# Moving the start of the projection phase two slots earlier in a fused threshold-attention and hard-swish kernel

## The chip, the cores and the metric

The kernel runs on one core of one Trainium2 chip. A core has five engines that run side by side and wait for one another through semaphores: TensorE (PE in the profile, its weight loads PEld), VectorE (DVE), ScalarE (ACT), GpSimd (POOL) and SyncE (SP, which here only issues transfers). The metric is the device time of one execution in microseconds (us). Less is better.

## What is computed

Threshold attention over 8 batches of 8 heads, 576 rows and 64 columns, and on its output, seen as 4608 tokens of 512 features, two projections with a hard-swish between them.

```python
scores = scale * np.matmul(q, k.transpose(0, 1, 3, 2))
thresh = np.max(scores, axis=-1, keepdims=True) - tau
scores = np.where(scores >= thresh, scores, -1000000000.0)
attn   = softmax(scores)                      # exp, divided by the sum of its row
x      = np.matmul(attn, v)                   # (8, 8, 576, 64) -> (4608, 512)
h      = x @ w_in                             # 512 -> 2048
g      = h * np.clip(h + 3.0, 0.0, 6.0) / 6.0
out    = g @ w_out                            # 2048 -> 512, float32
```

## The kernel before

The attention is cut into 16 groups of four heads ("quads", two pairs of heads each). A quad has nine slots. Slots 0 to 3 are 128 query rows of the first pair, 4 to 7 of the second pair, and slot 8 takes the last 64 rows of both. So there are 144 slots, n = 0 to 143, and one loop runs over them. In slot n each engine gets a share of a pipeline that is several slots deep:

- `scores(m)`: PE multiplies q and k in float32 into PSUM for a slot ahead.
- `sm_max(m)`: DVE copies the two score tiles out of PSUM and takes the row maxima; `sm_bias` on POOL makes the threshold.
- `sm_mask`, `sm_exp`: ACT masks and exponentiates, two instructions each for the two heads.
- `sm_recip` (DVE) and `sm_norm` (POOL): the quotient, in bfloat16, tile `pn`.
- the transposed `pn`: by `pe_transpose` where the slot is marked `on_chip` (nine PE instructions and a DVE copy), else by a DMA transpose that SP issues.
- `multiply(n)`: the products with v, on PE, and their copies `xT`, `xR` on DVE.
- `mm1(item)`: one piece of the first projection, eight PE instructions of 256 columns (or four of 512), and after it the rectifier `mm1_relu` (ACT in even slots, DVE in odd ones) and the gate `mm1_gate` (DVE).
- `second()`: pieces of the second projection. Four pieces of four PE instructions of 512 columns make one output tile of 128 tokens.

`N1` is the slot from which projections are done in the loop. There also the scores change from one slot at a time to bursts of two slots, in odd slots. Up to `N2` the exponentials of an even slot stand ahead of the rectifier on ACT.

```python
    N0 = 3
    N1 = 22
    N2 = 28
    HB, OB = 6, 7                 # PSUM banks of the two projections
    ...
    def bank():                   # two "small" banks, in turn: transposes and products with v
        nonlocal turn
        turn += 1
        return ps[:, (2, 5)[turn % 2], :]

    def copy_out(out, in_):
        if 0 <= now <= N1:
            nc.vector.tensor_copy(out=out, in_=in_)
        else:
            nc.scalar.copy(out=out, in_=in_)
    ...
    def first(n):                 # odd slots of the burst phase have score columns of their own
        return n > N1 + 2 and n % 2
    def score_col(n, a):
        return (704 if first(n) else 128) + (0 if a else 1536)
    ...
            sl.on_chip = len(queue) < N1 - 1 and (slot in (1, 3, 5, 7, 8) or slot == 0 and quad > 0)
    ...
    turns = {1: [("q", 1)], 2: [("k", 1)], 3: [("rest", 0)]}     # transposes of q and k by slot
    ...
        if quad < NB:             # NB = 2: when the products with v of the first two quads are done
            jobs = ((8, p0, 0, 512), (13 - 2 * quad, p1, 0, 512), (15 - 3 * quad, None, 0, 0))
        else:
            jobs = [(7 - quad % 2 + 2 * i, *of) for i, of in enumerate(
                ((p0, 0, 256), (p0, 256, 256), (p1, 0, 256), (p1, 256, 256), (None, 0, 0)))]
        for after, *of in jobs:
            products.setdefault(quad * NSLOT + after, []).append((quad, *of))

    def multiply(n):              # finished products bring pieces of the first projection into todo1
        copies = []
        for of, pair, *columns in products.get(n, ()):
            copies.append(av_rest(of) if pair is None else av_main(pair, *columns))
            if of % 2 and pair is None:
                todo1.extend(moe_of(of // 2)[1])
            elif pair == 2 * of + 1 and of % 2 and columns[0] == 0:
                todo1.extend(moe_of(of // 2)[0])
        return copies

    def second():
        nonlocal pieces, bb, mt, part
        pieces = 2 if now % 2 == 0 and todo2 else 0
        for _ in range(pieces):
            bb, mt, part = todo2.pop(0)
            mm2_part(bb, mt, part)
    ...
    for n, sl in enumerate(queue):
        ...
        if 0 < n <= N1: (exponentials of the slot before)
        if n <= N1 or n > N2 + 1 or n % 2 == 0: sm_max(queue[n + 1])
        even = n >= N1 and n % 2 == 0
        ...
        if N0 <= n <= N1: scores(n + 2)
        if even and n <= N2: sm_max(queue[n + 2])
        exp_first = even and n <= N2
        ...
        if todo1 and n >= N1:
            item, then = todo1.pop(0)
            ...
            h = mm1(item, 0 if n == len(queue) - 1 else OB if n > N1 and n % 2 and not pieces else HB)
            todo2.extend(then)
        ...
        elif n > N1 and n % 2:
            for m in (n + 3, n + 2): scores(m)
        ...
        if n < 4 or 15 < n < 20 or n > 33:
            start(vcasts, 1 if n < N1 or n % 2 else 0)
        else:                     # transfers of w_in and w_out, 32 pieces, issued by POOL
            start(casts, 2 if n in (5, 8, 11, 14) or 21 < n < 28 else 1)
    ...
    def last_out():               # the last output tile, one PSUM bank, two halves
        osb = o_pool.tile([P, d_model], F32, tag="osb", name="osb")
        r0, c = B * S - 64 - P, d_model // 2
        nc.scalar.activation(out=osb[:, 0:c], in_=o_ps[0][:, 0:c], func=Act.Copy, scale=1.0 / 6.0)
        nc.scalar.dma_start(out=out[r0:r0 + P, 0:c], in_=osb[:, 0:c])
        nc.vector.tensor_scalar_mul(out=osb[:, c:2 * c], in0=o_ps[0][:, c:2 * c], scalar1=1.0 / 6.0)
        nc.sync.dma_start(out=out[r0:r0 + P, c:2 * c], in_=osb[:, c:2 * c])
```

After the loop comes a tail: the pieces of both projections that are left over, most of them of the last batch, whose attention is only then complete.

Of the kernel before, what the change touches and what calls it, by code (L numbers as in the profile page):

```python
# [9 lines left out]
F32 = mybir.dt.float32  # L10
# [3 lines left out]
Act = mybir.ActivationFunctionType  # L14

P = 128
# [4 lines left out]
def kernel(  # L21
# [10 lines left out]
    nc = tc.nc  # L32
    B, H, S, D = q.shape
# [6 lines left out]
    NSLOT = 9  # L40
    NB = 2
    N0 = 3
    N1 = 22
    N2 = 28
    HB, OB = 6, 7
    scale = 1.0 / math.sqrt(D)
    tau = float(tau)
# [35 lines left out]
    def load_quad(quad):  # L83
        b, g = divmod(quad, 2)
        nat[quad] = (nat_pool.tile([P, 1152], F32, tag="nq", name="nq"),
                     nat_pool.tile([P, 4, 4, D], F32, tag="km", name="km"),
                     nat_pool.tile([P, 2 * D], F32, tag="kr", name="kr"))
        nq, km, kr = nat[quad]

        def main(dst, src, h, order, by=nc.sync):  # L90
            by.dma_start(out=dst[:, :, h, :], in_=src[b, 4 * g + h, 0:512, :].rearrange(order, t=4))

        def blocks_q(n, a, j):
            c = 32 * (2 * a + j)
            nc.sync.dma_start(out=nq[c:c + 32, n * S:(n + 1) * S].rearrange("p (k d) -> p k d", d=32),
                              in_=q[b, 4 * g + 2 * n + a, :, 32 * j:32 * j + 32].rearrange("(k r) d -> r k d", r=32))

        def blocks_k(n, a, j):
            c = 32 * (2 * a + j)
            nc.sync.dma_start(  # L100
                out=km[c:c + 32].rearrange("p t h d -> p (t h d)")[:, n * 512:(n + 1) * 512].rearrange(
                    "p (t m d) -> p t m d", t=4, d=32),
                in_=k[b, 4 * g + 2 * n + a, 0:512, 32 * j:32 * j + 32].rearrange("(m r t) d -> r t m d", r=32, t=4))

        def load_k(n):
            if b < NB:
                for a in range(2):
                    main(km, k, 2 * n + a, "(p t) d -> p t d")
            else:
                for a in range(2):  # L110
                    for j in range(2):
                        blocks_k(n, a, j)

        def load_q(n):
            if b < NB:
                for a in range(2):
                    main(nq[:, 0:1024].rearrange("p (t h d) -> p t h d", h=4, t=4), q, 2 * n + a, "(t p) d -> p t d",
                         by=nc.scalar if quad == n == 0 else nc.sync)
            else:
                for a in range(2):  # L120
                    for j in range(2):
                        blocks_q(n, a, j)

        def rest():
            for dst, src in ((kr[:], k), (nq[:, 1024:1152], q))[0:2 if b < NB else 1]:
                for n in range(2):
                    (nc.sync if b < NB else nc.gpsimd).dma_start(out=dst[64 * n:64 * n + 64, :].rearrange("p (h d) -> p h d", h=2),
                                      in_=src[b, 4 * g + 2 * n:4 * g + 2 * n + 2, 512:S, :].rearrange("h p d -> p h d"))

        def both():  # L130
            rest()
            load_k(1)

        if b < NB:
            loads.extend((lambda: load_k(0), lambda: load_q(0), rest, lambda: load_k(1), lambda: load_q(1)))
        else:
            loads.extend((lambda: load_q(0), lambda: load_k(0), lambda: load_q(1), both))
# [34 lines left out]
    def start(jobs, n):  # L172
        for _ in range(min(n, len(jobs))):
            jobs.pop(0)()
# [42 lines left out]


    def copy_out(out, in_):
        if 0 <= now <= N1:  # L220
            nc.vector.tensor_copy(out=out, in_=in_)
        else:
            nc.scalar.copy(out=out, in_=in_)  # L223
# [46 lines left out]
        return evict  # L270

    def first(n):
        return n > N1 + 2 and n % 2

    def score_col(n, a):
        return (704 if first(n) else 128) + (0 if a else 1536)
# [98 lines left out]
    def mm1(item, hb=HB):  # L375
        b, ni, c0 = item
        if c0 is None:
            for ki in range(KI):
                nc.tensor.matmul(ps[:, hb, :], xR[b // 2][:, ki, :], w_in_sb[:, ki, ni * P:ni * P + 512],  # L379
                                 start=(ki == 0), stop=(ki == KI - 1))  # L380
        else:
            for n in range(2):
                for ki in range(KI):
                    nc.tensor.matmul(ps[:, hb, n * 256:(n + 1) * 256], w_in_sb[:, ki, (ni + n) * P:(ni + n + 1) * P],  # L384
                                     xT[b][:, ki, c0:c0 + 256], start=(ki == 0), stop=(ki == KI - 1))
        return ps[:, hb, :]
# [27 lines left out]
    def mm2_part(bb, mt, part, ob=OB):  # L414
        if part == 0:
            o_ps[0] = ps[:, ob, :]
        for ni in range(part * 4, part * 4 + 4):
            nc.tensor.matmul(o_ps[0], gbuf[:, ni, mt * P:(mt + 1) * P], w_out_sb[:, ni, :],  # L418
                             start=(ni == 0), stop=(ni == NI - 1))
# [55 lines left out]
    for quad in range(NQUAD):  # L475
        for slot in range(NSLOT):
            sl = Slot()
            sl.quad, sl.slot, sl.n = quad, slot, len(queue)
            sl.on_chip = len(queue) < N1 - 1 and (slot in (1, 3, 5, 7, 8) or slot == 0 and quad > 0)
            queue.append(sl)  # L480
    scores(0)
    sm_max(queue[0])
    sm_bias(queue[0])
    scores(1)

    turns = {1: [("q", 1)], 2: [("k", 1)], 3: [("rest", 0)]}

    def turn_at(n, job, of):
        turns.setdefault(n, []).append((job, of))
# [10 lines left out]
    for quad in range(NQUAD):  # L500
        p0, p1 = 2 * quad, 2 * quad + 1
        if quad < NB:
            jobs = ((8, p0, 0, 512), (13 - 2 * quad, p1, 0, 512), (15 - 3 * quad, None, 0, 0))
        else:
            jobs = [(7 - quad % 2 + 2 * i, *of) for i, of in enumerate(
                ((p0, 0, 256), (p0, 256, 256), (p1, 0, 256), (p1, 256, 256), (None, 0, 0)))]
        for after, *of in jobs:
            products.setdefault(quad * NSLOT + after, []).append((quad, *of))
# [10 lines left out]

    def second():  # L520
        nonlocal pieces, bb, mt, part
        pieces = 2 if now % 2 == 0 and todo2 else 0
        for _ in range(pieces):
            bb, mt, part = todo2.pop(0)
            mm2_part(bb, mt, part)
# [5 lines left out]
    for n, sl in enumerate(queue):  # L531
# [45 lines left out]
        if todo1 and n >= N1:  # L577
            item, then = todo1.pop(0)
            if n == len(queue) - 2:
                second()  # L580
            h = mm1(item, 0 if n == len(queue) - 1 else OB if n > N1 and n % 2 and not pieces else HB)
            todo2.extend(then)
        else:
            item = None
# [61 lines left out]
        if n < 4 or 15 < n < 20 or n > 33:  # L646
            start(vcasts, 1 if n < N1 or n % 2 else 0)
        else:
            start(casts, 2 if n in (5, 8, 11, 14) or 21 < n < 28 else 1)
        prev = sl  # L650

    last = NQUAD - 1
    count = [1, 0 if todo2 and todo2[0][2] else 1]


    def last_out():
        osb = o_pool.tile([P, d_model], F32, tag="osb", name="osb")
        r0, c = B * S - 64 - P, d_model // 2
        nc.scalar.activation(out=osb[:, 0:c], in_=o_ps[0][:, 0:c], func=Act.Copy, scale=1.0 / 6.0)
        nc.scalar.dma_start(out=out[r0:r0 + P, 0:c], in_=osb[:, 0:c])  # L660
        nc.vector.tensor_scalar_mul(out=osb[:, c:2 * c], in0=o_ps[0][:, c:2 * c], scalar1=1.0 / 6.0)
        nc.sync.dma_start(out=out[r0:r0 + P, c:2 * c], in_=osb[:, c:2 * c])

    def rest1(item, then, on_act=True):
        h = mm1(item, hb=(0, 1, 3, 4)[count[0] % 4])
# [4 lines left out]
    def rest2():  # L670
        while todo2:
            bb, mt, part = todo2.pop(0)
            mm2_part(bb, mt, part, ob=OB - count[1] % 2)
            if part == 3:
                flush()
                if (bb, mt) == (B // 2 - 1, 8):
                    last_out()
                else:
                    late.extend(mm2_out(bb, mt, on_act=(count[1] % 2 == 0)))
                count[1] += 1  # L680

    av_main(2 * last + 1, 0, 256)()
# [50 lines left out]
```

## Time and profile before

| | |
|---|---|
| time, median of 3 runs | 516.75 us (516.36 to 516.82) |
| span of the profiled execution | 515.1 us |
| PE, PEld busy | 504.9, 318.6 us |
| DVE, ACT, POOL busy | 441.9, 451.8, 300.4 us |
| first and last reciprocal of the slot loop | 14.99 us, 469.15 us |

How to read it: each slot from 1 on does one reciprocal on DVE (`sm_recip` of the slot before), and one more follows the loop, so the starts of the 144 reciprocals cut the span into slots. The one done in slot n starts slot n in the tables of this document: slot 20 begins at 67.71 us, slot 22 at 73.53, slot 30 at 99.52, slot 36 at 119.69 and slot 46 at 151.66. The loop then ends near 469 us, and the rest is the tail. A busy share of the whole span mixes three stages (softmax alone, softmax with projections, projections alone), so the windows by slot say more than the totals. PE's busy time is modelled from the sizes of its instructions and counts overlapping ones once, so 100% does not mean that no more work would fit.

### The profile page before, as it was taken

What the parts mean: (1) busy time and instruction counts of PE and PEld (TensorE: products, weight loads), DVE (VectorE), ACT (ScalarE), POOL (GpSimd) and SP (SyncE); (2) the same over time, 40 slices, a digit from 0 to 9 for tenths busy, and PEclk for the clock granted to TensorE, in tenths of its full rate; (3) what the DMA queues carried; (4) which work ended last, traced back from release to release, by engine and by line L of the source; (5) the groups of instructions that cost most, each with busy time, mean ns of one, the idle gap of its engine ahead of it and who ended that gap; (6) DMA issues with size and microseconds to landing.
All of it is one profiled execution on the core that took longest, in us unless ns stands there. A gap on an engine that the chain in (4) does not pass through costs nothing.

```text
span 515.1 us, 12094 instructions
## 1 busy us (share of the span) xinstructions
PE 504.9 (98%) x4127; PEld 318.6 (62%) x4127; DVE 441.9 (86%) x1124; ACT 451.8 (88%) x980; POOL 300.4 (58%) x538
## 2 busy tenths in 40 slices
PE   8999999999999999999999999999999999999997
PEld 6655566566655666666655666666655666667563
DVE  3698898998999999999999999999999999887260
ACT  3999989999999999999999999999999999986060
POOL 0788888756666666666566756657566655552000
PEclk9999999999999999999999999999999999999999
DMA  6998999989999999999898999999999997655132
GB/s 140 163 175 140 157 148 178 160 141 176 164 195 157 173 164 170 179 176 174 164 178 143 183 169 160 159 170 168 164 173 176 183 181 114 115 111 81 74 63 61
DMA packets 314094, 78.77 MB, mean 153 GB/s; under 512 B 296624, under 2 KB 309168, under 8 KB 314032
## 3 DMA queue, kind: packets, MB, share of 16 engines
q1 hardware_dynamic: 294464, 67.90, 79.8%
q0 software_dynamic: 18368, 9.71, 15.6%
q8 instruction: 32, 0.52, 0.4%
q10 hardware_dynamic: 1200, 0.39, 0.3%
q14 instruction: 30, 0.25, 0.2%
HBM read 36.70 MB, written 9.44 MB: 90 GB/s over the span
## 4 chain that ended last, share of the span: by engine, by line
PE 79%; ACT 5%; DVE 2%; issue 0%
PE ps L288 24%; PE ps L418 24%; PE ps L384 20%; PE ps L349 7%; PE ps L379 3%; ACT s L317 2%; ACT s L312 2%; PE ps L352 1%; ACT r L392 1%; DVE g L407 1%; DVE r L394 0%; PE ps L340 0%; DVE s L303 0%; ACT kT L223 0%; PE ps L258 0%
## 5 line engine op out<-in xcount | busy, mean ns | idle before, releaser
L325 POOL TENSOR_SCALAR pn<-s,rinv 128x576 bf16<-128x576 f32 x288 | 211.4, 746 | 18.9 <-issue 4.8
L303 DVE TENSOR_SCALAR_CACHE_REDUCE s<-ps 128x576 f32<-128x576 f32 x288 | 205.0, 748 | 16.4 <-PE ps L288 8.3
L312 ACT ACTIVATE s<-s,bias 128x576 f32<-128x576 f32 x288 | 205.8, 762 | 5.1 <-POOL bias L308 4.7
L317 ACT ACTIVATE s<-s 128x576 f32<-128x576 f32 x288 | 192.4, 670 | 0.3
L288 PE MATMUL ps<-kT,qT 64*128 64x384 f32 (+7 forms) x1280 | 175.4, 419 | 3.9 <-DVE s L303 2.4
L288 PEld LDWEIGHTS ps<-kT,qT 64*128 64x128 f32 (+1 forms) x1280 | 102.9, 175 | 60.3 <-issue 15.8
L418 PE MATMUL ps<-w_out_sb,g 128*128 128x512 bf16 x576 | 134.1, 379 | 0.0
L384 PE MATMUL ps<-xT,w_in_sb 128*128 128x256 bf16 x1024 | 130.9, 273 | 0.8 <-DVE g L407 0.8
L384 PEld LDWEIGHTS <-w_in_sb 128*128 128x128 bf16 x1024 | 95.6, 98 | 40.7 <-issue 21.7
L308 POOL TENSOR_SCALAR bias<-m 128x2 f32<-128x2 f32 x144 | 27.1, 188 | 150.5 <-DVE rinv L320 135.6
L407 DVE SCALAR_TENSOR_TENSOR g<-r,ps 128x512 bf16<-128x512 f32 x128 | 87.8, 687 | 15.0 <-ACT r L392 10.8
L418 PEld LDWEIGHTS <-g 128*128 128x128 bf16 x576 | 56.2, 98 | 56.8 <-issue 0.4
L392 ACT ACTIVATE r<-ps,three 128x512 f32<-128x512 f32 x81 | 55.5, 686 | 24.7 <-PE ps L384 20.5
L317 ACT ACTIVATION_READ_ACCUMULATOR s<-s 128x1 f32 x288 | 54.4, 189 | 0.0
L394 DVE TENSOR_SCALAR r<-ps 128x512 f32<-128x512 f32 x63 | 42.9, 680 | 0.0
L349 PE MATMUL ps<-pT,vm 128*64 128x256 bf16 (+1 forms) x480 | 39.1, 285 | 0.0
L349 PEld LDWEIGHTS <-vm 128*64 128x64 bf16 x736 | 27.2, 110 | 16.1 <-issue 14.6
L360 DVE CAST xT<-ps 128x256 bf16<-128x256 f32 (+1 forms) x60 | 26.2, 436 | 10.2 <-PE ps L352 10.2
L426 DVE TENSOR_SCALAR osb<-ps 128x512 f32<-128x512 f32 x31 | 20.9, 673 | 8.4 <-PE ps L418 8.4
L303 DVE DVE_READ_ACCUMULATOR s<-ps 128x1 f32 x288 | 23.8, 83 | 0.0
L320 DVE RECIPROCAL rinv<-rsum 128x2 f32<-128x2 f32 x144 | 23.0, 159 | 0.6 <-ACT s L317 0.6
L144 POOL DMA_DIRECT2D vm<-in_v_dram x28 | 21.5, 768 | 0.7 <-issue 0.6
(57 smaller groups left out, 253.9 us busy)
## 6 DMA issues: line engine op xcount, KB each, us to landing
out_dram<-osb SPq DMA_DIRECT2D x31, 256.0 KB, 2.7
nq<-in_q_dram SPq DMA_DIRECT2D x96, 72.0 KB, 3.4
km<-in_k_dram SPq DMA_DIRECT2D x96, 64.0 KB, 3.4
vm<-in_v_dram POOLq DMA_DIRECT2D x24, 128.0 KB, 4.3
km<-in_k_dram SPq DMA_DIRECT2D x16, 128.0 KB, 4.1
w_in_sb<-in_moe_w_in_dram POOLq DMA_DIRECT2D x16, 128.0 KB, 3.6
w_out_sb<-in_moe_w_out_dram POOLq DMA_DIRECT2D x16, 128.0 KB, 4.2
pT<-pn SPq DMA_TRANSPOSE x117, 4.0
```

The lines of the kernel that those rows point to most:

```text
L288: nc.tensor.matmul(ps_flat[rows, c0:c0 + w], qT_of(pair)[a * 64:(a + 1) * 64, q0:q0 + rows.stop - rows.start], kT_of(pair)[a * 64:(a + 1) ...
L303: nc.vector.tensor_scalar(out=sl.s[:, i, :], in0=ps_flat[:, c0:c0 + S], scalar1=1.0, scalar2=None, op0=Alu.mult, op1=Alu.max, accum_out=sl ...
L308: nc.gpsimd.tensor_scalar(out=sl.bias[:], in0=sl.m[:], scalar1=-scale, scalar2=tau, op0=Alu.mult, op1=Alu.add)
L312: nc.scalar.activation(out=s, in_=s, func=Act.Prelu, bias=sl.bias[:, i:i + 1], scale=scale, alpha=REJECT)
L317: nc.scalar.activation(out=s, in_=s, func=Act.Exp, accum_out=sl.rsum[:, i:i + 1])
L325: nc.gpsimd.tensor_scalar(out=pn[:, i, :], in0=sl.s[:, i, :], scalar1=sl.rinv[:, i:i + 1], scalar2=1.0, op0=Alu.mult, op1=Alu.mult)
L349: nc.tensor.matmul(pb[a * 64:(a + 1) * 64, :], vm[:, 2 * hp + a, c * D:(c + 1) * D], pT[:, 5 * a + c, cols], start=(c == 0), stop=False)
L384: nc.tensor.matmul(ps[:, hb, n * 256:(n + 1) * 256], w_in_sb[:, ki, (ni + n) * P:(ni + n + 1) * P], xT[b][:, ki, c0:c0 + 256], start=(ki = ...
L392: nc.scalar.activation(out=r, in_=hps, func=Act.Relu, bias=three[:])
L394: nc.vector.tensor_scalar(out=r, in0=hps, scalar1=3.0, scalar2=0.0, op0=Alu.add, op1=Alu.max)
L407: nc.vector.scalar_tensor_tensor(out=out, in0=r, scalar=6.0, in1=hps, op0=Alu.min, op1=Alu.mult)
L418: nc.tensor.matmul(o_ps[0], gbuf[:, ni, mt * P:(mt + 1) * P], w_out_sb[:, ni, :], start=(ni == 0), stop=(ni == NI - 1))
```

## The change

It starts the burst scheme and the first projection in slot 20 in place of 22, and moves what hangs on it: the limit `N2`, the set of slots that are transposed on chip, the products of the second quad (one of them now in two halves), the rate at which the weights are fetched, and the number of pieces of the second projection in slots 36 to 44. Three further edits are independent of that: the k transpose of pair 1 moves from slot 2 to slot 1, the tail rows of k for quad 4 are fetched from SP's queue and not from POOL's, and the last output tile is computed as two halves of 256 columns in two PSUM banks. The purpose is to give PE projection work earlier, while the loop is still held up by the softmax.

```diff
-    N1 = 22
-    N2 = 28
+    N1 = 20
+    N2 = 26
...
-                    (nc.sync if b < NB else nc.gpsimd).dma_start(out=dst[64 * n:64 * n + 64, :] ...
+                    (nc.sync if quad < 5 else nc.gpsimd).dma_start(out=dst[64 * n:64 * n + 64, :] ...
...
     def copy_out(out, in_):
-        if 0 <= now <= N1:
+        if 0 <= now < N1 + 4:
...
-            sl.on_chip = len(queue) < N1 - 1 and (slot in (1, 3, 5, 7, 8) or slot == 0 and quad > 0)
+            sl.on_chip = len(queue) < N1 - 3 and (slot in (1, 3, 5, 7, 8) or slot == 0 and quad > 0)
...
-    turns = {1: [("q", 1)], 2: [("k", 1)], 3: [("rest", 0)]}
+    turns = {1: [("q", 1), ("k", 1)], 3: [("rest", 0)]}
...
         if quad < NB:
-            jobs = ((8, p0, 0, 512), (13 - 2 * quad, p1, 0, 512), (15 - 3 * quad, None, 0, 0))
+            jobs = (((8, p0, 0, 512), (9, p1, 0, 256), (12, p1, 256, 256), (14, None, 0, 0)) if quad else
+                    ((8, p0, 0, 512), (13, p1, 0, 512), (15, None, 0, 0)))
...
     def second():
         nonlocal pieces, bb, mt, part
-        pieces = 2 if now % 2 == 0 and todo2 else 0
+        pieces = min(len(todo2), {36: 3, 38: 1, 42: 1, 44: 1}.get(now, 2)) if now % 2 == 0 else 0
...
-            h = mm1(item, 0 if n == len(queue) - 1 else OB if n > N1 and n % 2 and not pieces else HB)
+            h = mm1(item, 0 if n == len(queue) - 1 else HB if n <= N1 or n % 2 == 0 or pieces > 1 else
+                    (2, 5)[turn % 2] if pieces else OB)
...
-            start(casts, 2 if n in (5, 8, 11, 14) or 21 < n < 28 else 1)
+            start(casts, 2 if n in (5, 8, 11, 14) or N1 <= n < N1 + 7 else 1)
...
-    def last_out():   (as above)
+    def last_tile(mt):
+        r0, c = B * S - 64 - P, d_model // 2
+        for half, by in enumerate((nc.scalar, nc.sync)):
+            o_half, columns = ps[:, (2, 5)[half], 0:c], slice(half * c, half * c + c)
+            for ni in range(NI):
+                nc.tensor.matmul(o_half, gbuf[:, ni, mt * P:(mt + 1) * P], w_out_sb[:, ni, columns],
+                                 start=(ni == 0), stop=(ni == NI - 1))
+            osb = o_pool.tile([P, d_model], F32, tag="osb", name="osb")
+            nc.vector.tensor_scalar_mul(out=osb[:, 0:c], in0=o_half, scalar1=1.0 / 6.0)
+            by.dma_start(out=out[r0:r0 + P, columns], in_=osb[:, 0:c])
...
     def rest2():
         while todo2:
             bb, mt, part = todo2.pop(0)
+            if (bb, mt) == (B // 2 - 1, 8):
+                flush()
+                last_tile(mt)
+                todo2.clear()
+                continue
             mm2_part(bb, mt, part, ob=OB - count[1] % 2)
```

More of the change, by code (lines that the diff above doesn't have):

```diff
@@ L126, in rest @@
                 for n in range(2):
-                    (nc.sync if b < NB else nc.gpsimd).dma_start(out=dst[64 * n:64 * n + 64, :].rearrange("p (h d) -> p h d", h=2),
+                    (nc.sync if quad < 5 else nc.gpsimd).dma_start(out=dst[64 * n:64 * n + 64, :].rearrange("p (h d) -> p h d", h=2),
                                       in_=src[b, 4 * g + 2 * n:4 * g + 2 * n + 2, 512:S, :].rearrange("h p d -> p h d"))
@@ L272, in first @@
     def first(n):
-        return n > N1 + 2 and n % 2
+        return n > N1 + 2 and n % 2 == 1
     def score_col(n, a):
@@ L653 @@
     count = [1, 0 if todo2 and todo2[0][2] else 1]
-    def last_out():
-        osb = o_pool.tile([P, d_model], F32, tag="osb", name="osb")
+    def last_tile(mt):
         r0, c = B * S - 64 - P, d_model // 2
[L659 to L662, printed above, removed]
+        for half, by in enumerate((nc.scalar, nc.sync)):
[6 more added lines that the diff above has]
+            by.dma_start(out=out[r0:r0 + P, columns], in_=osb[:, 0:c])
     def rest1(item, then, on_act=True):
@@ L675, in rest2 @@
                 flush()
[L676 to L679, printed above, removed]
+                late.extend(mm2_out(bb, mt, on_act=(count[1] % 2 == 0)))
                 count[1] += 1
```

## The prediction

> **What bounds the kernel now.** I read the totals first, then windows cut at the reciprocals of the slots, then the chain of waits for the length of single pieces of PE work, and the timeline for the end.
>
> ```profile
> PE 504.9 (98%) x4127; PEld 318.6 (62%) x4127; DVE 441.9 (86%) x1124; ACT 451.8 (88%) x980; POOL 300.4 (58%) x538
> ```
>
> The totals say PE, but three stages are mixed in them. The windows part them. Columns: stretch and its length, then busy us and instructions of PE, PEld, DVE, ACT, POOL, then PE's clock, DMA share, GB/s. In order: slots 10 to 19; 20 and 21; 22 and 23; 24 and 25; 26 and 27; 28 and 29; 30 and 31; 32 and 33; 34 and 35; 36 and 37; 38 and 39; 40 and 41; 42 and 43; 44 and 45.
>
> ```profile
> 40.50:67.71 27.21, 26.16 (x214) 15.77 (x213) 24.03 (x70) 26.73 (x61) 23.41 (x42) 1.00 1.00 152
> 67.71:73.53 5.82, 5.82 (x68) 3.77 (x67) 5.45 (x15) 5.12 (x11) 5.38 (x10) 1.00 0.88 122
> 73.53:80.76 7.23, 7.23 (x65) 4.95 (x64) 6.55 (x20) 6.13 (x15) 5.66 (x11) 1.00 1.07 166
> 80.76:87.24 6.48, 5.91 (x49) 3.94 (x47) 5.74 (x16) 6.45 (x15) 5.42 (x10) 1.00 1.03 172
> 87.24:93.20 5.96, 5.89 (x54) 3.94 (x53) 5.80 (x16) 5.96 (x14) 5.42 (x10) 1.00 1.03 177
> 93.20:99.52 6.32, 6.14 (x43) 3.65 (x42) 5.75 (x16) 6.32 (x15) 4.34 (x8) 1.00 1.25 158
> 99.52:105.98 6.46, 5.90 (x49) 3.90 (x48) 5.93 (x16) 6.40 (x16) 3.31 (x6) 1.00 1.08 159
> 105.98:112.97 6.99, 6.94 (x80) 4.18 (x78) 6.66 (x18) 6.20 (x14) 4.56 (x8) 1.00 0.83 144
> 112.97:119.69 6.72, 6.72 (x53) 4.29 (x52) 5.35 (x15) 6.34 (x15) 4.02 (x7) 1.00 0.86 155
> 119.69:126.04 6.35, 6.35 (x52) 4.06 (x50) 6.32 (x17) 5.88 (x14) 3.92 (x7) 1.00 1.04 175
> 126.04:132.23 6.19, 6.19 (x51) 4.06 (x50) 5.75 (x16) 5.82 (x13) 3.91 (x7) 1.00 1.18 176
> 132.23:138.62 6.39, 6.39 (x71) 3.97 (x70) 6.30 (x17) 6.33 (x16) 4.01 (x7) 1.00 0.91 153
> 138.62:145.15 6.53, 6.53 (x52) 4.17 (x51) 5.87 (x18) 6.22 (x14) 5.21 (x9) 1.00 1.26 163
> 145.15:151.66 6.51, 6.51 (x48) 3.79 (x47) 6.42 (x19) 6.14 (x15) 4.01 (x7) 1.00 1.14 190
> ```
>
> To slot 29 **ACT** sets the pace: 26.73 of 27.21 us, then 6.45 of 6.48, 5.96 of 5.96, 6.32 of 6.32. The one loss is the entry into the bursts, slots 22 and 23: 7.23 us with ACT at 6.13 and DVE at 6.55. From slot 32 **PE** has no gap, but ACT (5.8 to 6.3) and DVE (up to 6.42) stand close behind. The loop is nearly balanced, and work taken from PE alone buys little.
>
> The chain of waits gives lengths of PE work. Columns: start, us, what.
>
> ```profile
> 111.47 0.98 PE ps L384 x8
> 112.45 1.73 PE ps L418 x8
> ```
>
> A piece of the first projection is 0.98 us. Two pieces of the second are 1.73, so one is 0.865. The end, by the timeline:
>
> ```profile
> 511.27 0.38 ACT L659 ACTIVATE osb<-ps 128x256 f32<-128x256 f32 x1 [2.86 <-PE ps L418]
> 511.69 0.42 DVE L661 TENSOR_SCALAR osb<-ps 128x256 f32<-128x256 f32 x1 [6.63 <-ACT osb L659]
> 512.14 0.34 SPq L662 DMA_DIRECT2D out_dram<-osb  x1
> ```
>
> DVE's half starts only when ACT's has ended, though the columns are disjoint; 2.9 us after the last issue the span ends (515.06).
>
> **What the Trainium skill says.** "Perfetto Trace Analysis", Identifying the Most-Contended Engine: matmul busy time is a bad measure of how full PE is. The trace agrees: PE shows 5.82 of 5.82 us in slots 20 and 21, where it lacks the projections that it carries later in nearly the same time. So I count PE by work. The same page, Optimization Strategy, says that regimes with different most-contended engines gain from interleaving; that is the aim here, and no run of the kernel before shows its worth. "PSUM — Partial Sum Buffer", PSUM bank collisions raise a hardware error: two engines may not touch one bank and quadrant at once, disjoint columns included. That fits the serial halves at the end. "TensorE: Matmul & The Clock Gate", Back-to-back issue gap: N/2.4 + 2.5 ns, so 216 ns for 512 columns; the trace has 1.73/8 = 216. For 256 it gives 109, the trace 0.98/8 = 122; I use 122.
>
> **The change part by part.** First what the lists of pieces do. The first batch has 16 pieces of the first projection. Before, they fill slots 22 to 37, and the next pieces, which `multiply(37)` adds, follow from 38. After, they fill 20 to 35; quad 3's products have not moved, so slots 36 and 37 have none, and from 38 on all is as before. The second projection starts in slot 28 in place of 30. To slot 45 it does 16 pieces in both: before 2 in each even slot; after 2 in 28, 30, 32, 34, then 3, 1, 2, 1, 1. **So the lead of two slots is given back by slot 46**, and the gain is only what lies between 20 and 45, plus start and end.
>
> Slots 20, 21. Added: rectifier on ACT (0.69), one on DVE (0.68), two gates (2 x 0.69). Gone from DVE: two copies of on-chip transposes (2 x 0.74), and 0.67 - 0.42 for the product split in halves; come in from slot 22: a kT copy (0.68). DVE 5.45 + 0.68 + 1.38 - 1.48 - 0.25 + 0.68 = 6.46; ACT 5.12 + 0.69 = 5.81. With the entry loss of before (7.23 - 6.55 = 0.68) 7.1 us, +1.3.
>
> Slots 22, 23: no entry now, DVE 6.55 - 0.74 - 0.68 + 2 x 0.28 = 5.69 (the kT tail copies come over from ACT), ACT 6.13 - 0.53 = 5.60. I take 6.0, as slots 26 and 27 have: -1.2.
>
> Slots 24 to 27 keep their order and are ACT-bound: 0. Slots 28 to 35 now carry both projections. A window 36 slots later, where the same products recur, shows that load in steady state: slots 64 to 71 take 6.38 + 6.50 + 6.81 + 6.37 = 26.06 (209.80 to 235.86), against 6.32 + 6.46 + 6.99 + 6.72 = 26.49 now. As the passage into that load may itself cost, I take half: -0.2.
>
> Slots 36, 37: PE 6.35 - 2 x 0.98 + 0.865 = 5.26; ACT 5.88 - 0.69 = 5.19; DVE loses two gates, a rectifier and an output copy, to 3.6. I take 5.4: -0.95. Slots 38 to 41: one piece less in 38, and the output copy (0.67) now falls in 39 and not in 41. PE 12.58 - 0.87 = 11.71, ACT 12.15, DVE 12.05; I take 12.3: -0.3. Slots 42, 43: PE 5.66, ACT 6.22, so 6.25: -0.3. Slots 44, 45: DVE stays at 6.42, so 6.45: -0.05. Together -1.6, though PE sheds 2 x 0.98 + 2 x 0.865 = 3.7 us here.
>
> Start. In slot 2 a kT copy stands at 17.75 on DVE and the scores behind it begin at 18.47; the next maximum on DVE, at 19.84, waited 1.43 us for them. With the transposes a slot earlier that wait shrinks, but ACT has no gap from 15.78 to 21.1, so I credit 0.25.
>
> End. 32 instructions of 256 columns replace 16 of 512: 32 x 0.122 - 16 x 0.216 = +0.46 on PE. ACT's half ahead of DVE's (0.42) goes, and the first half's transfer is out of the last one's way. I take -0.05.
>
> The transfers of weights and k rows, and three more DMA transposes (slots 17 to 19, which are used four or more slots later), sit beside POOL at 5.4 of 5.8 us and below, and cost nothing.
>
> Sum: +1.3 - 1.2 - 0.2 - 1.6 - 0.25 - 0.05 = -2.0 us, so **514.7 us**.
>
> **The rivals.** (a) The work moved forward costs as much as it saves. For it: ACT and DVE carry all of it, both are over 5.1 of 5.8 us in slots 20 and 21, and the pieces come back to the old places by slot 46. Against: slots 36 and 37 lose a rectifier, gates and matmuls on three engines at once. It would make 516 to 517. (b) PE is the true bound from slot 32 on and the whole 3.7 us come back: 513 or a little less. Against: ACT at 5.8 to 6.3 us of every pair of slots. (c) A new wait. Splitting one product flips the turn of the two small banks for the rest of the loop, and in slots 39, 43 and 45 the first projection sits in a small bank that odd slots' scores share; the earlier entry also meets the loads of the second batch's v. With some 49 pairs of slots behind slot 46, 0.03 us a pair is already 1.5 us, in either direction. In the pairs shown PE has no gap that a bank could explain, so I expect little; at worst 518. (d) The last tile loses its 0.46 without a return: +0.5.
>
> **Range and chances.** Terms 20 to 35 are good to 0.7, 36 to 45 to 0.5, the bank turn to 0.8, start and end to 0.3; together about 1.2 us, so 513.0 to 516.6 eight times in ten. A 2% change would be 10.3 us, which nothing here can make: 0.01 faster, 0.98 within, 0.01 slower.
>
> **What would show it.** Right: slot 36 starts about 0.35 us earlier than 119.69 (the start term included), slots 36 and 37 take about 5.4 us with ACT full, slot 46 starts about 2 us earlier than 151.66, the distance from there to the last reciprocal (317.5 us) is unchanged, and the last PE instruction ends 0.4 to 0.5 us later against the last reciprocal, but not the span. Wrong: slots 20 to 23 over 13.6 us, PE waiting in odd slots for copies out of banks 2 and 5, or a changed pace behind slot 46.

## The result and the profile after

The changed kernel takes **519.51 us** (median of 3 runs, 519.31 to 520.68) against 516.75: the ratio is 1.0062, with a 95% interval of 1.0037 to 1.0086. It is slower by 2.8 us, and 2.9 us above the top of the predicted range. The profiled spans are 515.1 us before and 517.7 us after.

The totals show almost nothing:

```profile
PE 505.2 (98%) x4126; PEld 320.6 (62%) x4126; DVE 441.5 (85%) x1125; ACT 450.8 (87%) x977; POOL 298.1 (58%) x536
```

So the windows again, cut at the reciprocals of the changed kernel. Columns as before. In order: slots 20 and 21; 22 and 23; 24 and 25; 26 and 27; 28 and 29; 30 and 31; then 36 and 37; 38 and 39; and 46 and 47.

```profile
66.81:75.33 8.52, 7.87 (x62) 5.06 (x60) 6.62 (x17) 7.10 (x16) 5.45 (x10) 1.00 1.26 162
75.33:81.22 5.89, 5.03 (x62) 3.24 (x62) 5.80 (x18) 5.61 (x13) 5.41 (x10) 1.00 1.12 158
81.22:87.19 5.97, 5.32 (x46) 3.74 (x46) 5.75 (x18) 5.97 (x16) 2.89 (x6) 1.00 1.16 146
87.19:94.76 7.57, 6.63 (x51) 4.86 (x52) 5.82 (x18) 5.04 (x11) 6.86 (x13) 1.00 1.27 230
94.76:101.67 6.91, 6.34 (x51) 4.04 (x50) 5.86 (x18) 6.61 (x15) 4.35 (x9) 1.00 1.30 170
101.67:108.23 6.56, 6.56 (x53) 4.31 (x52) 6.47 (x17) 6.50 (x16) 3.31 (x6) 1.00 0.73 138
...
121.75:126.90 5.15, 5.15 (x41) 3.58 (x40) 4.04 (x13) 4.61 (x11) 3.91 (x7) 1.00 1.14 224
126.90:133.48 6.58, 6.04 (x47) 4.11 (x45) 6.36 (x17) 5.74 (x14) 3.89 (x7) 1.00 1.12 129
...
153.23:159.93 6.70, 6.70 (x49) 3.90 (x48) 5.86 (x18) 6.33 (x14) 3.99 (x7) 1.00 1.12 219
```

Set beside the windows before, this is where the time went:

| stretch | before | after | difference | predicted |
|---|---|---|---|---|
| start to slot 20 | 67.71 | 66.81 | -0.90 | -0.25 |
| slots 20, 21 | 5.82 | 8.52 | +2.70 | +1.3 |
| slots 22, 23 | 7.23 | 5.89 | -1.34 | -1.2 |
| slots 24 to 27 | 12.44 | 13.54 | +1.10 | 0 |
| slots 28 to 35 | 26.49 | 26.99 | +0.50 | -0.2 |
| slots 36 to 47 | 38.21 | 38.18 | -0.03 | -1.6 |
| slot 48 to the last reciprocal | 311.25 | 311.25 | 0.00 | 0 |
| last reciprocal to the end | 45.91 | 46.55 | +0.64 | -0.05 |

Three stretches stand out, and each has a wait of its own in the trace.

**Slots 26 and 27: a late DMA transpose.** The waits between 80 and 100 us (who waited <- for what: us in all, times, the longest):

```profile
POOL pn L325 <- DMA pT<-pn: 3.1, 1, 3.1
ACT s L312 <- POOL bias L308: 2.5, 1, 2.5
...
DVE s L303 <- POOL pn L325: 1.7, 1, 1.7
...
PE ps L349 <- DMA pT<-pn: 0.8, 1, 0.8
```

POOL could not write the `pn` of slot 24, because the `pn` pool has four buffers (`bufs=4` in the kernel) and the transpose of slot 20 had not yet read the one it needed. The wait then passed to ACT, DVE and PE. SP's own timeline shows why that transpose was late. After:

```profile
70.58 2.35 SPq L95 DMA_DIRECT2D nq<-in_q_dram  x4
73.03 3.37 SPq L333 DMA_TRANSPOSE pT<-pn  x1
76.45 1.36 SPq L127 DMA_DIRECT2D kr<-in_k_dram  x2
77.85 2.66 SPq L100 DMA_DIRECT2D km<-in_k_dram  x4
80.61 1.40 SPq L333 DMA_TRANSPOSE pT<-pn  x1
```

Before, the same stretch of SP's queue ended in

```profile
73.68 6.85 SPq L333 DMA_TRANSPOSE pT<-pn  x3
```

Slot 20's `pn` was finished at 72.34 us after and at 73.23 before. Its transpose was issued 8.27 us later after (80.61) and 0.45 us later before (73.68), and landed at 87.38 and 78.15. After, from 70.58 us on SP goes from one issue to the next with less than 0.2 us between them: in slots 18 to 25 it began 26.2 us of issuing in 26.0 us, before 17.6 in 25.2. Three transposes (slots 17 to 19) and two transfers of k rows have been added to it.

**Slots 38 to 47: PE waits in the burst.** PE's timeline in slot 39; the bracket is the idle time and its releaser:

```profile
128.82 2.29 PE L288 MATMUL ps<-kT,qT 64*128 64x384 f32 x14
131.66 0.70 PE L288 MATMUL ps<-kT,qT 64*128 64x256 f32 x2 [0.54 <-DVE g L407]
```

The last two score instructions need the columns of the small bank in which the first projection of slot 39 still stands, until DVE's gate has read it. Slot 45 shows the same 0.54 us.

**Slots 20 and 21: the entry.** The chain of waits there:

```profile
72.49 0.61 DVE kT L221
73.15 0.75 PE ps L288 x4
73.97 1.44 DVE s L303 x4
```

A copy of a transposed k on DVE holds the bank of the second half of the burst; the maxima of the next slot wait for it in turn (DVE idle for 0.88 us).

### The profile page after: what moved, and what is told of

Same layout as the page of the kernel before. It is cut to its first block, busy times and chain, and to the rows that moved or that the text cites. A ratio compares the mean times of both kernels' runs of the same rounds, so it can differ in the third digit from the quotient of the medians.

```text
span 517.7 us, 12082 instructions
## 1 busy us (share of the span) xinstructions
PE 505.2 (98%) x4126; PEld 320.6 (62%) x4126; DVE 441.5 (85%) x1125; ACT 450.8 (87%) x977; POOL 298.1 (58%) x536
## 4 chain that ended last, share of the span: by engine, by line
PE 79%; DVE 5%; DMA 2%; ACT 2%; POOL 0%; issue 0%; POOLq 0%; DVEq 0%
PE ps L288 25%; PE ps L418 23%; PE ps L384 19%; PE ps L349 7%; PE ps L379 2%; DVE g L407 1%; PE ps L352 1%; DMA pT<-pn 1%; DVE s L303 1%; DMA g<-go 1%; DVE r L394 1%; PE ps L663 1%; ACT r L392 1%; ACT s L312 1%; ACT s L317 0%
## 5 line engine op out<-in xcount | busy, mean ns | idle before, releaser
L288 PE MATMUL ps<-kT,qT 64*128 64x192 f32 (+7 forms) x1280 | 177.4, 419 | 3.4 <-DVE s L303 1.9
L288 PEld LDWEIGHTS ps<-kT,qT 64*128 64x128 f32 (+1 forms) x1280 | 104.7, 175 | 59.4 <-issue 15.6
L418 PE MATMUL ps<-w_out_sb,g 128*128 128x512 bf16 x560 | 131.0, 379 | 0.0
L418 PEld LDWEIGHTS <-g 128*128 128x128 bf16 x560 | 54.5, 98 | 55.3 <-issue 0.7
```

What stands on the lines that cost most here:

```text
L288: nc.tensor.matmul(ps_flat[rows, c0:c0 + w], qT_of(pair)[a * 64:(a + 1) * 64, q0:q0 + rows.stop - rows.start], kT_of(pair)[a * 64:(a + 1) ...
```

## The experiments

Each time is a median, with its lowest and highest run; ratios are to the kernel before, timed beside it on the same chip (516.6 to 517.1 in the four sessions). "After" is the changed kernel.

### The small bank

```diff
-            h = mm1(item, 0 if n == len(queue) - 1 else HB if n <= N1 or n % 2 == 0 or pieces > 1 else
-                    (2, 5)[turn % 2] if pieces else OB)
+            h = mm1(item, 0 if n == len(queue) - 1 else HB if n <= N1 or n % 2 == 0 or pieces else OB)
```

> The changed kernel, but in slots 39, 43 and 45 the first projection stays in bank 6 and doesn't go to a small bank (2 or 5). Theory (bank): in these slots the last two score matmuls of the burst, which lie in banks 2 and 5, stand behind the DVE gate that empties the small bank (gaps of 0.54 us on PE in slots 39 and 45). Slots 38 to 47 then go from 33.03 us (126.90 to 159.93) back to about 31.9, as in the kernel before (31.86); the whole gets about 1.1 us shorter. Rival (the uneven number of pieces, 3-1-2-1-1, is itself the cause, or bank 6 waits as long): slots 38 to 47 stay at 32.7 or more.

Measured: 518.22 us (517.66 to 518.85), ratio 1.0024 (1.0014 to 1.0035). Slots 38 to 47 take 32.04 us, against 33.02 after and 31.86 before. The pairs 38 and 39, and 46 and 47:

```profile
127.20:133.78 6.58, 5.95 (x49) 3.83 (x47) 6.36 (x19) 6.27 (x15) 3.90 (x7) 1.00 1.23 142
...
153.07:159.24 6.17, 6.17 (x47) 3.65 (x46) 5.76 (x16) 5.80 (x13) 4.00 (x7) 1.00 1.02 187
```

The small bank costs 1.0 us, and rival (c) is right there. But without it these slots are still 0.2 us over before, not 0.65 under.

### k rows back to POOL's queue

```diff
-                    (nc.sync if quad < 5 else nc.gpsimd).dma_start(out=dst[64 * n:64 * n + 64, :] ...
+                    (nc.sync if b < NB else nc.gpsimd).dma_start(out=dst[64 * n:64 * n + 64, :] ...
```

> The changed kernel, but quad 4's tail rows of k are issued by POOL again and not by SP. Theory (SP's queue is full): SP's issues take 26.2 of the 26.0 us of slots 18 to 25; with two issues (1.31 us) gone, the transpose of slot 20 is issued and lands about 1.3 us earlier, POOL's wait for its buffer (3.1 us in slot 25) shrinks by as much, and slots 26 and 27 go from 7.57 to about 6.3. Rival (the DMA engines are full, because the weights come two pieces a slot from slot 20): the same bytes move, so no change within 0.3 us. Rival (POOL is short of time): it gets slower.

Measured: 519.51 us (516.22 to 525.39), ratio 1.0053 (1.0029 to 1.0078). In the profile the transpose of slot 20 is issued 2.23 us earlier (78.38), and slots 26 and 27 take 6.06 us, as the theory of SP's queue has it. But the median is that of after, the runs spread over 9.2 us, and in the profile slots 28 to 31 take 17.51 us against 13.47 after:

```profile
PE ps L349 <- DMA pT<-pn: 2.4, 1, 2.4
...
PE ps L418 <- DMA w_out_sb<-in_moe_w_out_dram: 1.9, 1, 1.9
```

Four transposes here needed 9.7 to 11.2 us from issue to landing (after: 4.5 to 7.5). The wait had only moved. The Trainium skill, "DMA: Bandwidth & Descriptors", Issuing engines are not separate DMA queues, says that transfers issued by several engines share the same 16 DMA engines, and that a second issuing engine saves only issue time, usually small. The first half agrees with this run. The second does not hold in this case: in slots 18 to 25 of after SP began 26.2 us of issuing in 26.0 us.

### Slot 17 transposed on chip again

```diff
-            sl.on_chip = len(queue) < N1 - 3 and (...)
+            sl.on_chip = len(queue) < N1 - 2 and (...)
```

> The changed kernel, but slot 17 is still transposed on chip (nine PE instructions and a 0.74 us DVE copy in place of one DMA transpose). Theory (SP's queue is full): one transpose of 1.3 to 2.6 us leaves the queue, so slots 26 and 27 go from 7.57 to about 6.3; the DVE copy adds up to 0.7 us in slots 19 to 21. Rival (DMA engines full): the landing of the transposes of slots 19 and 20 stays at 5 to 7 us after issue and the wait in slot 25 stays over 2.5 us.

Measured: 516.68 us (516.27 to 517.66), ratio 0.9996 (0.9988 to 1.0005). The transpose of slot 20 is issued at 77.34, 3.3 us earlier than after, and lands at 84.50, just ahead of POOL's need:

```profile
77.34 3.96 SPq L333 DMA_TRANSPOSE pT<-pn  x2
```

It took 7.16 us to land, no less than after (6.77), so the gain is in the moment of issue. SP is still almost full: 25.4 us of issuing begun in the 26.0 us of slots 18 to 25. Slots 26 and 27:

```profile
87.14:93.20 6.06, 5.92 (x50) 4.22 (x51) 5.82 (x16) 5.72 (x13) 4.97 (x10) 1.00 1.29 222
```

Slots 26 to 31 take 18.95 us (21.05 after, 18.74 before), slots 20 and 21 stay at 8.52: the copy that this puts back on DVE costs nothing there. In the median one transpose less gives back the whole loss of the change, though the loss in the small bank is still in it (slots 38 to 47: 32.94 us).

### The k transpose of slot 21 moved to slot 20

```diff
-                    ... else first_odd + (0, 2, 3, 5, 7)[i], job, of)
+                    ... else first_odd + (0, 1, 3, 5, 7)[i], job, of)
```

> The changed kernel, but the k transpose of quad 3's first pair is done in slot 20 and not in 21, so that its DVE copy comes at the start of slot 21 and not at its end. Theory (entry): in slot 21 the scores of slot 23 wait in their small bank for that copy, DVE then waits 0.88 us for the scores and ACT 0.99 us for the projection behind them; with the copy earlier, slots 20 and 21 go from 8.52 to about 7.6 us. Rival (the entry is long because DVE and ACT wait for PE work that is put in anyway): 8.3 or more, or PE waits for the rows of k, which land at 69.6 us.

Measured: 518.48 us (517.97 to 519.83), ratio 1.0036 (1.0025 to 1.0047). Slots 20 and 21 take 7.95 us: 0.57 of the entry's loss was the k copy, and 0.85 above the predicted 7.1 stays. In slots 26 to 31 (21.31 us) the wait of this execution is PE's, 1.54 us for `w_out_sb` in slot 30.

### The k transpose of pair 1 alone, in the kernel before

```diff
-    turns = {1: [("q", 1)], 2: [("k", 1)], 3: [("rest", 0)]}
+    turns = {1: [("q", 1), ("k", 1)], 3: [("rest", 0)]}
```

> The kernel before with one part of the change alone: the k transpose of pair 1 in slot 1 and not in 2. Theory: this part gains by itself and keeps it; from the first reciprocal to that of slot 4 it takes 8.23 us as in the changed kernel and not 8.77, and every later slot takes what it takes before, so 0.5 us less in all. Rival: the gain is eaten in the ACT-bound slots to 21, and the reciprocal of slot 20 comes no earlier against the first one than before (52.72 us).

Measured: 516.11 us (515.84 to 516.75), ratio 0.9986 (0.9979 to 0.9993). From the first reciprocal to slot 4 it takes 8.24 us in place of 8.77, and nothing else moves: this edit alone is worth 0.5 us.

### The old end in the changed kernel

The changed kernel with `last_out` and `rest2` of the kernel before.

> The changed kernel with the last output tile as before: one bank, 512 columns, halves by ACT and DVE in turn. From the last reciprocal to the end of the span the kernel before takes 45.91 us and the changed one 46.55. Theory: the two banks are no loss; 0.25 us more on PE against 0.42 us less of waiting behind it, and the rest of the 0.64 is a late transposed tile of the projection, which landed 4.8 us after its issue and not 3.4. So 45.8 to 46.4 here, by chance of that transpose. Rival: the halves of 256 columns cost the whole difference, and it falls to 45.9 while that transpose is as late as in the changed kernel.

Measured: 520.63 us (518.88 to 521.54), ratio 1.0072 (1.0051 to 1.0093). From the last reciprocal to the end it takes 46.41 us, though PE's last instruction ends 42.09 us behind the last reciprocal as in the kernel before (there the end was at 45.91): from the issue of the last transfer to the end of the span it takes 3.42 us here and 2.91 before, and a single profile does not settle the end. Slots 26 to 31 have the same code as after and took 23.27 us here; slots 26 and 27 took 6.06 of them, without after's wait. PE's timeline in slot 30:

```profile
103.06 0.38 PE L418 MATMUL ps<-w_out_sb,g 128*128 128x512 bf16 x1 [2.69 <-DMA w_out_sb<-in_moe_w_out_dram]
```

### Weights fetched two slots later

```diff
-            start(casts, 2 if n in (5, 8, 11, 14) or N1 <= n < N1 + 7 else 1)
+            start(casts, 2 if n in (5, 8, 11, 14) or N1 + 1 < n < N1 + 9 else 1)
```

> The changed kernel, but the weights come one piece a slot in slots 20 and 21 and two a slot in 22 to 28. Theory (SP's queue is full): the weights are issued by POOL, so the transpose of slot 20 is issued at about 80.6 us as before, and slots 26 and 27 stay over 7 us. Rival (the DMA engines are full of weights): with two pieces fewer before slot 22 the transposes of slots 19 to 21 land in under 5 us and slots 26 and 27 go to about 6.1. Both may hold in part: the run without SP's two issues of k rows moved the wait to slots 28 to 31, where transposes took up to 11 us to land.

Measured: 524.8 us (520.52 to 527.81), ratio 1.0151 (1.0085 to 1.0217). Slots 26 and 27 take 6.18 us, but the last piece of `w_out` lands 3.4 us after slot 30 has begun (after: 0.9 us ahead of it), and slots 30 and 31 take 10.63. Fetching later relieves the transposes and starves the second projection, which now begins in slot 28.

### Both repairs

Slot 17 on chip and the first projection in bank `HB`, the two edits above together.

> The changed kernel with both repairs: slot 17 on chip, and no projection in a small bank. If the two causes are separate, the gains add: slots 24 to 29 as with slot 17 on chip alone (18.3 us), slots 38 to 47 32.0 us, the last reciprocal 1.0 us earlier than with slot 17 alone, the time about 515.7 us, which is under the kernel before. Rival: the place of the transfers shifts again and a wait appears in slots 28 to 33; then 517 or more.

Measured: 516.6 us (515.32 to 517.86), ratio 0.9997 (0.9988 to 1.0006). Slots 26 to 31 take 18.94 and 38 to 47 31.95 us: the repairs add up there. But the median is no shorter than with slot 17 alone (516.68), where 515.7 was expected: the 1.0 us of the bank is seen in the windows and not in the whole time. In this profile one transpose in slot 55, outside the change, came late and cost 1.05 us.

### Repairs, earlier k transpose, earlier weights

The last kernel with the edit of slot 20, and

```diff
-            start(casts, 2 if n in (5, 8, 11, 14) or N1 <= n < N1 + 7 else 1)
+            start(casts, 2 if n in (5, 7, 8, 10, 11, 13, 14) or N1 <= n < N1 + 7 else 1)
```

> The changed kernel with four repairs: slot 17 on chip, no projection in a small bank, quad 3's first k transpose in slot 20, and three of the weight pieces moved ahead to slots 7, 10 and 13. If the causes are separate and all repaired: slots 20 and 21 7.95 us, slots 26 to 31 18.9, slots 38 to 47 32.0, so about 0.6 us less than with the first two repairs alone, 515.5 to 516.0 us in all and steady over its runs. Rival (any early entry costs what it gains): 516.5 or more.

Measured: 515.57 us (514.61 to 517.28), ratio 0.9979 (0.9963 to 0.9995). It beats both kernels, by 0.2% against the kernel before, though its six runs spread over 2.7 us.

### The three transposes by DMA, in the kernel before

```diff
-            sl.on_chip = len(queue) < N1 - 1 and (...)
+            sl.on_chip = len(queue) < N1 - 5 and (...)
```

> The kernel before with one part of the change alone: slots 17, 18 and 19 transposed by DMA and not on chip. Theory (it is the meeting of more DMA traffic with an earlier need of the weights): here the weights have two slots more, so at most the wait for a transposed tile in slots 25 to 27 appears, +0 to 1.5 us, less three DVE copies. Rival (the three DMA transposes alone make the loss): slots 26 to 31 take 20 us or more, as in all runs of the changed kernel with three more DMA transposes (20.2 to 23.6), and not 18.7.

Measured: 517.68 us (515.85 to 523.35), ratio 1.0038 (1.0014 to 1.0062). Its profile happens to show no loss (slots 26 to 31: 18.75 us), but its runs spread over 7.5 us, where those of the kernel before, beside them, spread over 1.9. The transposes alone, without the earlier burst, cost 1.1 us in the median, and scatter the time.

### Earlier weights alone

> The changed kernel, but with three pieces of the weights moved ahead of slot 16 (slots 7, 10 and 13 issue two). Theory (late weights): the last piece is issued two slots sooner, TensorE has no wait for the weights in slots 28 to 31, and the spread of the run times narrows to about a microsecond; slots 26 to 31 at most 20.3. Rival (the transposes alone): a wait for a transposed tile in slots 25 to 27 stays, 1 us or more.

Measured, with the weights' edit of two sections above put into the changed kernel: 520.49 us (518.97 to 522.73), ratio 1.0076 (1.0052 to 1.0099). There is no wait for `w_out`, whose last piece lands 5.8 us ahead of slot 30, but slots 26 to 31 take 20.84 us: POOL waits 2.9 us for the `pn` buffer of slot 24 and goes on at 87.54, 0.18 us after the transpose of slot 20 has landed, and PE waits 1.15 us for `pT`. The weights were not the cause of that wait.

### The second projection held back to slot 30

```diff
-        pieces = min(len(todo2), {36: 3, 38: 1, 42: 1, 44: 1}.get(now, 2)) if now % 2 == 0 else 0
+        pieces = 2 if now % 2 == 0 and now >= N1 + 10 and todo2 else 0
```

> The changed kernel, but the second projection starts in slot 30 and not in 28, two pieces in each even slot, as before; so its weights are needed two slots later, and nothing goes to a small bank in slots 39 to 45. Theory (late weights and small bank): no wait for weights, slots 26 to 31 20.3 or less, slots 38 to 47 31.9; the time under 518. Rival (the transposes alone): a wait of over 1 us in slots 25 to 27 stays, and the time stays near 519.

Measured: 518.11 us (516.73 to 520.46), ratio 1.003 (1.002 to 1.004). Nothing goes to a small bank any more either, since no slot has a single piece. Slots 26 to 31 take 18.59 us in the profile. Slots 26 and 27, whose code is still that of after, take 6.07 of them and not 7.57. Slots 38 to 47 take 32.50 us where 31.9 was expected, behind 4.83 in 36 and 37. The runs spread over 3.7 us; where the slower ones lose their time is not shown.

### Which part of the best kernel repairs

The best kernel without the earlier weights:

> As the version with four repairs (515.57 us), but the weights again in the change's own order. Theory: the three pieces of weights moved ahead are worth nothing by themselves, since with slot 17 on chip the transfers keep up; slots 20 and 21 7.95, 26 to 31 18.9, 38 to 47 32.0 us, the time 515.5 to 516.0. Rival: without them TensorE waits for weights in slots 28 to 31 in some executions, and the runs spread over more than 3 us or the median is over 516.2.

Measured: 516.04 us (515.21 to 517.72), ratio 0.9985 (0.9977 to 0.9993). Slots 26 to 31 take 18.95 us, without a wait. With slot 17 on chip the weights need not come earlier.

The kernel before with only the k transpose of pair 1 and the new last tile:

> The kernel before with the two parts of the change that hang on nothing else: the k transpose of pair 1 in slot 1 and the last output tile in two banks. Theory: the first gives 0.5 to 0.7 us by itself (516.11 us measured with it alone); the second costs 0.0 to 0.1 us on TensorE and spares the 0.42 us of ACT's half, so 0.3 us: about 515.8. The last reciprocal to the end of the span takes 45.6 us and not 45.9. Rival (the halves of 256 columns cost more than the wait): 516.2 or more.

Measured: 515.94 us (515.47 to 516.5), ratio 0.9981 (0.9972 to 0.9990). From the last reciprocal to the end it takes 45.51 us against 45.91. **In the medians, two edits that have nothing to do with the shift give all that the repaired shift (516.04) gives.** The profiles differ a little: from the first reciprocal to the end of the span the repaired shift takes 498.48 us and the two edits 499.12. With runs that spread over 2.5 and 1.0 us, the medians do not settle such a difference.

### A rectifier taken from DVE at the entry

```diff
-            mm1_gate(item, h, mm1_relu(h, on_act=even))
+            mm1_gate(item, h, mm1_relu(h, on_act=even or n == N1 + 1))
```

> The version with four repairs, and the rectifier of slot 21 on ACT and not on DVE. What is left of the long entry: slots 20 and 21 still take 7.95 us there, where 7.1 was predicted. Theory (TensorE's order): DVE waits at 73.3 us for the scores of the burst, and TensorE has worked without a gap from 68.0, so taking 0.68 us from DVE changes nothing within 0.15 us. Rival (DVE is the entry's bound, as the prediction had it): slots 20 and 21 fall to 7.5 or less.

Measured, in the best kernel: 517.1 us (515.92 to 520.16), ratio 1.0007 (0.9994 to 1.0019). The windows of slots 20 and 21, of the best kernel and then of this one:

```profile
66.73:74.69 7.96, 7.45 (x62) 5.26 (x61) 7.11 (x20) 7.12 (x16) 5.45 (x10) 1.00 1.28 162
```

```profile
67.95:75.91 7.96, 7.45 (x62) 5.26 (x61) 6.41 (x19) 6.91 (x15) 5.45 (x10) 1.00 1.26 159
```

DVE loses 0.70 us of work and the pair of slots keeps its 7.96. DVE's sum does not set this stretch. (The median is 1.1 us above that of the repaired shift without the earlier weights, timed beside it; the profile does not show why.) What PE does meanwhile in the best kernel, with no idle bracket on any line:

```profile
68.03 1.05 PE L384 MATMUL ps<-xT,w_in_sb 128*128 128x256 bf16 x8
68.92 0.60 PE L233 MATMUL ps<-identf,km 128*128 128x128 f32 x4
69.36 1.04 PE L384 MATMUL ps<-xT,w_in_sb 128*128 128x256 bf16 x8
70.32 0.63 PE L349 MATMUL ps<-pT,vm 128*64 128x256 bf16 x8
...
70.99 2.21 PE L288 MATMUL ps<-kT,qT 64*128 64x384 f32 x16
```

The scores that DVE needs next come last in this row, behind two pieces of the projection, and DVE then waits 0.47 us for them. With the rectifier gone from DVE the wait grows to 1.20:

```profile
74.55 0.76 DVE L303 TENSOR_SCALAR_CACHE_REDUCE s<-ps 128x576 f32<-128x576 f32 x1 [1.20 <-PE ps L288]
```

## Why the prediction was wrong, step by step

**The transfers "cost nothing": this step failed, and it was the costliest.** The prediction set "three more DMA transposes" and the k rows beside POOL's load and left SP out. But SP began 26.2 us of issuing in the 26.0 us of slots 18 to 25, so slot 20's transpose was issued 8.27 us after its data were ready, and the slack of "four or more slots" is just the depth of the `pn` buffers: slot 24 writes where slot 20 is read. In the profile of after slots 26 to 31 lose 2.3 us (21.05 against 18.74) where -0.1 or so was expected. With slot 17 on chip they took 18.94 or 18.95 us in each of five kernels. Seven of the eight shifted kernels without it, after included, took 20.2 to 23.6. A full queue alone is not the loss: with slot 17 on chip SP still began 25.4 us of issuing in 26.0; what counts is whether the transpose of slot 20 lands before slot 24 needs its buffer. There is a second edge at the same place: the second projection moved two slots forward and the last transfer of its weights only one (issued in slot 28, before in 29), so their lead shrank from 3.8 us (before, slot 32) to 0.9 (after, slot 30), and it fails in some executions. Nor does each execution have the wait in slots 26 and 27: two runs with the same code up to slot 28 took 6.06 and 6.07 us there. That is also why single profiles of the same code name different culprits.

**Slots 38 to 45, "I expect little" of the bank: failed.** Rival (c) named the shared bank and the sign that would show it; the mistake was to dismiss it because the profile before shows no such wait. It could not: that wait needs the new placing of the first projection. It cost 1.0 us.

**Slots 38 to 45, the gain of 0.65: failed also.** With the bank repaired, slots 38 to 47 take 31.95 to 32.04 us against 31.86. Taking pieces from PE there bought nothing, with ACT at 6.27 and DVE at 6.36 of 6.58 us in slots 38 and 39. The part "36 and 37" was right: 5.15 us, predicted 5.4. So of the 1.6 us forecast for slots 36 to 47, 1.0 came once the bank was left alone (37.19 us against 38.21).

**Slots 20 and 21, +1.3: mis-sized, and its step failed.** It took 8.52 us in place of 7.1. The working added up DVE (6.46) and an entry loss carried over from slots 22 and 23. The k copy on DVE was 0.57 of the difference. For the rest the last experiment excludes DVE's sum; that PE's order sets it is read from the timeline, and no run changed that order. Slots 22 and 23 were right (5.89, predicted 6.0).

**Slots 24 to 35.** The prediction gave 24 to 27 as 0 and 28 to 35 as -0.2. Where no transfer is late, with slot 17 on chip, the shift costs 0.2 us in slots 26 to 31 and gains 0.5 in 24 and 25 (5.96 against 6.48) and 0.5 in 32 to 35 (13.18 against 13.71): -0.8 in all, more than predicted. In after the same slots lost 1.6 us.

**The start, -0.25: right in kind, too small.** The edit gives 0.54 us; the other 0.36 of the table is the moment at which the first reciprocal could start, which differs between executions of all these kernels (14.45 to 15.77 us).

**The end, -0.05: right in kind, too small, and hidden in the profile.** The last two copies no longer wait for one another. In the seven kernels with the new end in which PE was not held up, the last transfer is issued 42.62 to 42.68 us behind the last reciprocal; in the four with the old end it is 43.0. So some 0.4 us is gained. From that issue to the end of the span the profiles show 2.7 to 3.4 us with either end, which is why the whole distance overlaps: 45.5 to 46.0 us with the new end, 45.7 to 46.4 with the old. After itself took 46.55, 0.64 more than before: PE's last rows waited 0.53 us for a transfer of `g` that landed 4.82 us after its issue (3.44 before), and the stretch behind the last issue was 0.49 us longer. That DVE's last copy now waits for PE alone is seen in the timeline:

```profile
513.88 0.42 DVE L666 TENSOR_SCALAR osb<-ps 128x256 f32<-128x256 f32 x1 [1.32 <-PE ps L663]
```

The +0.46 on PE did not appear: where `g` was in time PE's last instruction ends 42.13 to 42.19 us behind the last reciprocal, 42.09 before.

**The turn of the small banks behind slot 46: no effect.** From slot 48 to the last reciprocal both kernels take 311.25 us.

So the sum of -2.0 us failed by 4.7 in the profile: 2.5 us in slots 24 to 35 and at the end, most of it where transfers came late; 1.6 in slots 36 to 47; 1.3 in slots 20 to 23; and 0.65 the other way at the start. Rival (a) holds for what is left, as far as the medians can tell: even repaired, the shift gives 516.04 us where its two independent edits alone give 515.94.

**What stays open.** How the late landing divides between SP's queue and the DMA engines behind it. Moving k rows off SP brought the first transpose 2.2 us forward and left others at 10 to 11 us, so the queue is not all of it. Nor does one transpose less cure it for good: with slot 17 on chip a transpose was late in slot 55 of one profile, and one run reached 520.16 us. A fifth `pn` buffer would tell the two apart further and was not tried; transposes issued from another engine were not tried either.

## What to carry to other kernels

An engine that only issues transfers has a budget as well: add up the issue times in the stage against its length, and set the time to landing against the number of buffers until the first reuse, before calling a transfer hidden. Work shifted to an earlier stage has to bring its operands' transfers forward with it, or its lead over them is the price. And an edit that claims a shared bank has to be judged by who else uses that bank, not by a profile in which it is not yet shared.

## What was not expected of the hardware

**PE's clock fell after a short gap.** In the run with the old end, PE stood idle for 2.69 us in slot 30. A window of 1 us behind that gap; the clock is the third number from the end:

```profile
104.00:105.00 1.00, 1.00 (x7) 0.46 (x7) 0.17 (x1) 0.98 (x4) 0.88 (x2) 0.50 1.21 260
```

The clock was 0.50 for 3.4 us, and eight instructions of the first projection took 1.65 us in place of 1.05. The run with later weights did the same after gaps of 1.85 and 0.42 us; gaps of 2.39 and 1.88 us (k rows on POOL) and 1.54 us (k transpose in slot 20) left it at 1.00. The Trainium skill, "TensorE: Matmul & The Clock Gate", HAM oscillation — how this bites in real kernels, gives gaps over some 3.4 us as the limit; the measurement decides, and here shorter ones were enough. What decides between the gaps that did it and those that did not, no run shows. In the runs where it happened, a late transfer was paid twice.

**A DMA transpose of one slot has no fixed time.** For the same `pT` the issue on SP took 1.24 to 5.06 us and the landing 3.15 to 11.2 us, over all profiles. The longest are those of the run with the k rows on POOL's queue; what sets the time is not shown.
